# Chunk 3's attention value product as a Strassen product in two 64-row streams, with six squares on ScalarE

## The chip, the cores and the metric

One core of a Trainium2 chip runs the whole program. The metric is the time of one execution on the device in microseconds (us). The profile comes from one execution more, recorded by the hardware profiler; its instructions are told by engine: PE is TensorE's matmuls, PEld its weight loads, DVE is VectorE, ACT is ScalarE, POOL is GpSimd, SP is SyncE, which here issues DMAs.

## The reference

Eight batches of 3008 tokens. `u` and `v` have 256 channels, `z` has 64.

```python
scores = (1.0 / S) * np.matmul(z, z.transpose(0, 2, 1))
attn = np.maximum(scores, 0.0) ** 2
out = np.matmul(attn, v)
x = (u * out).reshape(B * S, D)                 # 24064 x 256
h = x @ w_in                                    # 256 x 2048
g = h * (1.0 / (1.0 + np.exp(-1.702 * h)))
y = g @ w_out                                   # 2048 x 256
```

The score matrix of a batch is symmetric, since both of its factors are `z`.

## The kernel before, in words

**Tiling.** A batch has 24 key blocks of 128 tokens (the last holds 64) and 6 query chunks of 512 tokens (`NCH = 6`, `CH = 512`; the last has 448 for some purposes). Two key blocks are one unit, so a unit `(i, jp)` is the scores of query chunk `i` against key blocks `2 jp` and `2 jp + 1`: a tile of 128 x 2 x 512. Only units on and above the diagonal are computed. What lies below it comes out of them by a DMA transposition (`turn_unit`, issued on SP's queue), whose result lies in `TT[b, i, cj]`, four blocks by four blocks. The unit on the diagonal is folded: its second half is transposed into the tile `ad`.

**A unit's way.** `scores` has PE make a pair of 64-row matmuls (line 247) into a PSUM tile of pool `ps2` (two buffers); `square` has ScalarE apply Relu into `rl` (line 268, 258 or 263) and VectorE square it into `a` (lines 282, 285, 273, 259, 264); then the DMA transposition follows. `take(b, n)` does this for the next `n` units of the queue. `SCHED` says at which step `n` of which chunk a unit is taken: during chunk `i`, mostly units of chunk `i + 1`, and the order inside a chunk comes from `pieces`.

**The value product.** `attend(b, i)` gives the list of steps of chunk `i`. In chunks 0 to 3 and 5, the 128 rows of PE are used as two halves of 64 rows, `TOP` and `LOW`, which work at the same time. A step is a pair of matmuls of 64 rows by 512 columns (line 529): first channel half 0 from the top rows and channel half 1 from the low rows over 23 key blocks, then the last block's half, then the same with the halves exchanged; 47 pairs. The two halves write different PSUM banks (pool `ps1`, four banks). When they exchange banks, PE must know that the other half's last matmul has landed: `post` puts an instruction on POOL that waits for it, and `behind` makes the next matmul wait for that instruction. At the end of a chunk, two gates (line 546) multiply the two banks with the transposed `u` on VectorE and give `XT[b, i]`.

**Chunk 4** of batches 1 to 6 (`split`) is already a Strassen product in Winograd's form: `attend_split` runs seven products `P1` to `P7`, each over three pairs of key chunks `t` (line 440, 128 rows by 256 columns), into three PSUM banks. `P6`, `P7` and `P4` are accumulated on the bank of `P1`, and `P3` on that of `P5`, after a copy or an addition has taken the value so far out. The sums of values `VT` (`value_forms`, line 363) and of scores `SA` (`score_forms`, lines 383 to 396: `S1` to `S4`) are made on VectorE at the steps that `fills` lists as `(chunk, step)`.

**The second part.** From step 2 of chunk 4, `up_group` interleaves the first 16 groups of the up product (line 584): PE makes `hg`, ScalarE applies Gelu into `gf` (line 597, two buffers), and the scaling of `gf` into `g` is VectorE's (line 603) or in some groups ScalarE's (line 601). The other groups and the down product, again a Strassen product (line 757), follow after chunk 5. `store` transposes a result on VectorE (line 859) and writes it with four DMAs on SP. `turn_u` transposes `u` on VectorE (line 214), at the steps that `TURNS` lists; `load_u` loads it through POOL's queue.

**Order.** All five engines' orders are written out by hand: an engine runs its instructions in the order in which the program issues them, and a tile pool of n buffers makes the first writer of a buffer wait for the last reader of the tile before.

Of the kernel before, what the change touches and what calls it, by code (L numbers as in the profile page):

```python
# [11 lines left out]
P = 128  # L12
# [3 lines left out]
def kernel(  # L16
# [210 lines left out]
    def folded(b, i):  # L227

        return i < NCH - 1 and b > 0
# [5 lines left out]
    def scores(b, group):  # L235
        scs = []
        zt = ZT[b]
        for i, jp in group:
            sc = ps2.tile([P, 2, CH], F32, name="sc", tag="ps2")
            turn = turned(b, i) and jp >= NU - 2  # L240
            kp, qi = (2 * i + jp - (NU - 2), NCH - 1) if turn else (jp, i)
            q0, q1 = qi * CH, qi * CH + width(qi)
            if jp == 2 * i + 1 and (folded(b, i) or i == NCH - 1):
                q0 += CH // 2
            for r in range(2):
                h = slice(r * DQK, (r + 1) * DQK)
                pe.matmul(  # L247
                    sc[:, r, :q1 - q0], zt[h, 2 * kp + r, :], zt[h].rearrange("d n p -> d (n p)")[:, q0:q1],
                    start=True, stop=True,
                )  # L250
            scs.append(sc)
        return [lambda u_=u_, sc=sc: square(b, *u_, sc) for u_, sc in zip(group, scs)]

    def square(b, i, jp, sc):
        rl = pw.tile([P, 2, CH], F16, name="rl", tag="rl", bufs=3)
        if folded(b, i) and jp == 2 * i + 1:
            rh = rl[:, :, :CH // 2]
            act.activation(rh, sc[:, :, :CH // 2], AF.Relu, scale=csc)
            dve.tensor_tensor(unit[b, i, jp][:, 1], rh, rh, ALU.mult)
            return  # L260
        if i == NCH - 1 and jp == NU - 1:
            n = LAST - CH // 2
            act.activation(rl[:, :, :n], sc[:, :, :n], AF.Relu, scale=csc)
            dve.tensor_tensor(unit[b, i, jp][:, :, CH // 2:LAST], rl[:, :, :n], rl[:, :, :n], ALU.mult)
            return
        turn = jp >= NU - 2 and (turned(b, i) or i == NCH - 1)
        n = width(NCH - 1 if turn else i)
        act.activation(rl[:, :, :n], sc[:, :, :n], AF.Relu, scale=csc)  # L268
        if folded(b, i) and jp == 2 * i:
# [11 lines left out]
        unit[b, i, jp] = a  # L281
        dve.tensor_tensor(a[:, :, :n], rl[:, :, :n], rl[:, :, :n], ALU.mult)  # L282
        if turn:
            twice = rl[:, :, LFULL:LAST]
            dve.tensor_tensor(a[:, :, LAST:], twice, twice, ALU.mult)
        if i == NCH - 1 and jp == NU - 2:
# [13 lines left out]


    ORDER0 = [(0, 1), (0, 2), (1, 2), (0, 3), (1, 3), (2, 3), (0, 4), (1, 4), (2, 4), (3, 4)]
    squared = {}
# [62 lines left out]

    def score_part(b, t, e, part, m):

        i, c0 = NCH - 2, 2 * t + e
        if c0 == i:  # L370
            if part == 0:
                return unit[b, i, 2 * i][:, 2 * m:2 * m + 2]
            return unit[b, i, 2 * i + 1][:, m].rearrange("p r (q c) -> p r q c", c=P)
        tile_ = TT[b, min(c0, i), max(c0, i)][:, 2 * m:2 * m + 2]
        if t < NCH // 2 - 1:
            return tile_.rearrange("p q g c -> p (q g c)")
        tile_ = tile_[:, :, 2 * part:2 * part + 2]
        return tile_ if part == 0 else tile_.rearrange("p q r c -> p r q c")

    def score_form(b, t, name, part):  # L380
        a11, a12, a21, a22 = (score_part(b, t, e, part, m) for m, e in ((0, 0), (0, 1), (1, 0), (1, 1)))
        if name == "S3":
            dve.tensor_tensor(a21, a11, a21, ALU.subtract)
            return
        if (t, name) not in SA:
            SA[t, name] = pa.tile([P, 2, CH], F16, name="sa", tag="a", bufs=26)
        if t < NCH // 2 - 1:
            view = lambda x: SA[t, x].rearrange("p r c -> p (r c)")
        else:
            view = lambda x: SA[t, x][:, part].rearrange("p (q r c) -> p q r c", r=2, c=P)  # L390
        if name == "S1":
            dve.tensor_tensor(view(name), a21, a22, ALU.add)
        elif name == "S2":
            dve.tensor_tensor(view(name), view("S1"), a11, ALU.subtract)
        else:
            dve.tensor_tensor(view(name), a12, view("S2"), ALU.subtract)

    def score_forms(b, t):
        parts = 1 if t < NCH // 2 - 1 else 2
        return [lambda x=x, p_=p_: score_form(b, t, x, p_) for x in ("S1", "S2", "S4", "S3") for p_ in range(parts)]  # L400

    def moving(b, t, g, name):

        raw = {"P1": (0, 0), "P2": (0, 1), "P4": (1, 1), "P7": (1, 0)}
        if name in raw:
            m, e = raw[name]
            i, c0 = NCH - 2, 2 * t + e
            if c0 != i:
                return TT[b, min(c0, i), max(c0, i)][:, 2 * m:2 * m + 2, g]
            if g < 2:  # L410
                return unit[b, i, 2 * i][:, 2 * m:2 * m + 2, g]
            return unit[b, i, 2 * i + 1][:, m, g % 2]
        form = SA[t, {"P5": "S1", "P6": "S2", "P3": "S4"}[name]]
        if t < NCH // 2 - 1:
            return form.rearrange("p r c -> p (r c)").rearrange("p (q g c) -> p q g c", g=CB, c=P)[:, :, g]
        part = form[:, g // 2].rearrange("p (q r c) -> p q r c", r=2, c=P)
        return part[:, :, g % 2] if g < 2 else part[:, g % 2]

# [7 lines left out]
    def attend_split(b, i):  # L426

        seq = [("P1", 0), ("P1", 1), ("P1", 2), ("P5", 0), ("P5", 1), ("P2", 0), ("P2", 1), ("P6", 0), ("P6", 1)]
        seq += [("P5", 2), ("P6", 2), ("P3", 0), ("P3", 1), ("P7", 0), ("P7", 1), ("P7", 2)]
# [4 lines left out]
        def step(name, t, h):  # L434
# [4 lines left out]
            for g in (2 * h, 2 * h + 1):  # L439
                pe.matmul(  # L440
                    bank, still(b, t, g, name), moving(b, t, g, name),
                    start=new and (t, g) == (0, 0), stop=(t, g) == (2, CB - 1), skip_group_check=True,
                )
# [20 lines left out]
        return [lambda x=x, t=t, h=h: step(x, t, h) for x, t in seq for h in range(2)]  # L464

    def fills(b):

        VT.clear()
        SA.clear()
        at = {(0, 19): [lambda: pool.tensor_copy(VZ[TOP], V16[b][TOP, NJ - 1])]}  # L470
        slots = [(0, n) for n in (20, 23, 26, 28)] + [(1, n) for n in (27, 31, 35, 39, 43)]
        slots += [(2, n) for n in (19, 21, 23)]
        ops = [op for t in range(3) for op in value_forms(b, t)]
        slots += [(2, n) for n in (28, 33, 38, 43)] + [(3, n) for n in (30, 34, 41, 44)]
        slots += [(4, n) for n in (8, 9, 11, 12, 14, 15, 17, 18)]
        ops += [op for t in range(3) for op in score_forms(b, t)]
        assert len(ops) == len(slots)
        for where, op in zip(slots, ops):
            at.setdefault(where, []).append(op)
        return at  # L480
# [88 lines left out]
    def up_group(b, q):  # L569
# [28 lines left out]
        if pair and q >= LAGY:  # L598
            some_sums(3 if q % 2 else 8)
        if q >= LAGY and q % 8 in (1, 3, 5):  # L600
            act.activation(g, gf[:, :, :n], AF.Copy, scale=FSC)  # L601
        else:
            dve.tensor_scalar(g, gf[:, :, :n], FSC, None, ALU.mult)  # L603
# [273 lines left out]
    def pieces(b, i):  # L877
# [6 lines left out]
        if split(b, i):  # L884
            return [lst[0], lst[3], lst[2], lst[1]]
        k = max(len(lst) - 6, 2)
        return lst[:k] + lst[-2:] + lst[k:-2]
# [3 lines left out]
        0: {n: 1 for n in (5, 9, 13, 17, 30, 33, 36, 39, 42, 45)} | {NJ: 2},  # L891
        1: {n: 1 for n in (5, 9, 13, 17)} | {NJ: 2},
        2: {n: 1 for n in (2, 7, 12, 17)} | {NJ: 2},
        3: {n: 1 for n in (3, 10, 17, 38)} | {NJ: 2},
        4: {},
# [7 lines left out]
    TURN = {(1, NJ + 4): 2, (2, NJ + 4): 3, (4, 10): 4, (5, 8): 5}  # L903
    TURNS = {(1, NJ + 4): 2, (2, NJ + 4): 3, (4, 20): 4, (5, 8): 5}
    LOADW = {
# [18 lines left out]
    def take(b, n):  # L924
        for post_ in scores(b, [queue.pop(0) for _ in range(n)]):
            post_()

# [22 lines left out]
    copies = first_zt(2)  # L950
    posts[0]()
    first_cast(3)
    posts[1]()
    take(0, 1)
# [4 lines left out]
    for b in range(B):  # L959
# [7 lines left out]
        for i in range(NCH):  # L967
# [4 lines left out]
            if i == 0 and split(b, NCH - 2):  # L972
                extra = fills(b)
            for n, step in enumerate(attend_split(b, i) if split(b, i) else attend(b, i, b == 0 and i == 0)):
                if b == 0 and i == 0 and n in (5, 24):
# [9 lines left out]
                if (i, n) in turn:  # L985
                    turn_u(b, turn[i, n])
                if (i, n) in ((3, 4), (4, 1) if more else (4, 14)) and LAST2:
                    LAST2.pop(0)()
# [92 lines left out]
```

## Time and profile before

| | |
|---|---|
| median of 3 runs | 1170.55 us (1170.28 to 1172.03) |
| the profiled execution's own time | 1170.41 us |
| its span, first to last instruction | 1168.5 us |
| PE busy | 1161.9 us, 8212 matmuls |
| VectorE busy | 958.7 us, 1596 instructions |
| ScalarE busy | 842.1 us, 959 instructions |
| POOL busy | 224.3 us |
| DMA transpositions into `tt` | 232 issues, 3.4 us from issue to landing in the median |

The page gives an engine's busy time as a share of the span, and cuts the span into 40 slices with the granted clock of TensorE. Busy times of matmuls overlap (each is shown longer than the distance to the next), so the pace of PE is read from the starts of instructions that follow each other. A chain of waits is followed back from the last instruction of the program. Batch 2, whose chunks 0 to 4 lie between 303.5 and 372.8 us of the span, serves as the example.

### The profile page before, as it was taken

The page shows a single profiled execution, that of the slowest core. Times are in us where ns is not written, and L with a number is a line of the kernel's source. Part 1 is how long each engine was busy: PE and PEld are TensorE (multiplying, and loading weights), DVE is VectorE, ACT ScalarE, POOL GpSimd, SP SyncE. Part 2 cuts the span into 40 slices and gives each one's busy share as a digit, 9 for nine tenths or more (in the row PEclk, how much of TensorE's full clock was granted, in tenths as well). Part 3 has the DMA queues.
Part 4 walks back from the last instruction along what each step waited for, and adds up shares of the span by engine and source line. Part 5 has one row for each costly group of instructions (what it writes and reads, how often), then busy time and mean ns, then how long its engine had stood idle before and what let it go on. Part 6 is the DMA issues. An engine that isn't in the chain of part 4 may idle for free.

```text
span 1168.5 us, 21541 instructions
## 1 busy us (share of the span) xinstructions
PE 1161.9 (99%) x8212; PEld 589.5 (50%) x8212; DVE 958.7 (82%) x1596; ACT 842.1 (72%) x959; POOL 224.3 (19%) x307
## 2 busy tenths in 40 slices
PE   9999999999999999999999999999999999999998
PEld 3544455544455445554445545555444554544446
DVE  7789878988788886889868897789977899664876
ACT  7888864788647886478864787658867588672785
POOL 3033200432004320042101431024210251001000
PEclk9999999999999999999999999999999999999999
DMA  9996399754996559875498755987559965697023
GB/s 225 202 155 107 79 172 158 105 91 92 166 158 103 91 109 172 146 111 87 96 173 146 114 88 109 170 149 104 87 107 174 145 108 81 123 162 139 1 37 73
DMA packets 459033, 143.54 MB, mean 123 GB/s; under 512 B 424624, under 2 KB 453040, under 8 KB 458928
## 3 DMA queue, kind: packets, MB, share of 16 engines
q1 hardware_dynamic: 402464, 102.36, 52.4%
q0 software_dynamic: 55104, 38.49, 21.1%
q8 instruction: 64, 1.05, 0.4%
q10 hardware_dynamic: 1360, 1.31, 0.4%
q14 instruction: 41, 0.34, 0.1%
HBM read 60.29 MB, written 24.64 MB: 73 GB/s over the span
## 4 chain that ended last, share of the span: by engine, by line
PE 99%; ACT 1%; issue 0%; DVE 0%
PE o L529 36%; PE hg L584 28%; PE st L757 23%; PE sc L247 6%; PE oz L440 5%; PE st L805 1%; PE yp L731 1%; ACT rl L268 0%; PE w L101 0%; ACT ZT L145 0%; PE zp L137 0%; DVE y L823 0%; ACT zst L128 0%; DVE nil L76 0%
## 5 line engine op out<-in xcount | busy, mean ns | idle before, releaser
L597 ACT ACTIVATE gf<-hg 128x1024 f32<-128x1024 f32 (+1 forms) x384 | 383.8, 1003 | 116.3 <-PE hg L584 100.5
L268 ACT ACTIVATE rl<-sc 128x1024 f16<-128x1024 f32 (+1 forms) x301 | 288.6, 992 | 153.7 <-PE sc L247 112.8
L584 PE MATMUL hg<-xt,W 128*128 128x512 f16 (+1 forms) x1408 | 353.5, 374 | 0.0
L529 PEld LDWEIGHTS <-V 64*128 64x128 f16 (+1 forms) x3810 | 205.9, 94 | 202.7 <-POOLq L88 6.6
L529 PE MATMUL o<-a,V 64*128 64x512 f16 (+3 forms) x2254 | 290.2, 368 | 0.4 <-DVE a L282 0.4
L603 DVE TENSOR_SCALAR gt<-gf 128x1024 f16<-128x1024 f32 (+1 forms) x288 | 203.1, 708 | 72.0 <-ACT gf L597 70.1
L282 DVE TENSOR_TENSOR a<-rl 128x1024 f16<-128x1024 f16 (+1 forms) x266 | 175.9, 672 | 80.1 <-ACT rl L268 79.0
L584 PEld LDWEIGHTS <-W 128*128 128x128 f16 x1536 | 149.6, 98 | 155.7 <-issue 2.6
L207 POOL DMA_DIRECT2D uq<-in_u_dram x168 | 120.7, 728 | 341.1 <-DVE ut L214 157.6
L529 PE MATMUL o<-tt,V 64*128 64x512 f16 (+1 forms) x1278 | 166.9, 376 | 0.1
L247 PE MATMUL sc<-ZT 64*128 64x512 f16 (+3 forms) x688 | 117.0, 356 | 0.6 <-ACT ZT L145 0.3
L757 PEld LDWEIGHTS <-WT 128*128 128x128 f16 x736 | 72.0, 98 | 79.5 <-issue 0.6
L601 ACT ACTIVATE gt<-gf 128x1024 f16<-128x1024 f32 (+1 forms) x96 | 98.1, 1021 | 3.1
L757 PE MATMUL st<-gt,W 128*128 128x512 f16 (+1 forms) x368 | 89.9, 370 | 0.0
L757 PE MATMUL st<-s,WT 128*128 128x512 f16 (+1 forms) x368 | 89.1, 370 | 0.0
L757 PE MATMUL st<-gt,WT 128*128 128x512 f16 (+1 forms) x368 | 88.7, 370 | 0.0
L993 POOL COPY hold<-tt 128x2 f16<-128x2 f16 x6 | 1.4, 230 | 430.1 <-DMA tt<-a 287.4
L757 PEld LDWEIGHTS <-W 128*128 128x128 f16 x552 | 53.8, 98 | 58.2
L774 DVE SCALAR_TENSOR_TENSOR y<-st,y 128x512 f32<-128x512 f32 (+1 forms) x69 | 45.8, 663 | 19.7 <-PE st L757 18.8
L721 DVE TENSOR_TENSOR s<-s,gt 128x1024 f16<-128x1024 f16 (+1 forms) x92 | 60.5, 657 | 0.8
L723 DVE TENSOR_TENSOR s<-gt,s 128x1024 f16<-128x1024 f16 (+1 forms) x92 | 59.4, 662 | 2.0 <-DVE s L721 0.9
L719 DVE TENSOR_TENSOR s<-gt 128x1024 f16<-128x1024 f16 (+1 forms) x92 | 60.2, 659 | 0.9
(101 smaller groups left out, 975.7 us busy)
## 6 DMA issues: line engine op xcount, KB each, us to landing
out_dram<-yo SPq DMA_DIRECT2D x156, 128.0 KB, 2.8
uq<-in_u_dram POOLq DMA_DIRECT2D x140, 128.0 KB, 3.5
V<-in_v_dram POOLq DMA_DIRECT2D x35, 256.0 KB, 6.1
tt<-a SPq DMA_TRANSPOSE x232, 3.4
uq<-in_u_dram POOLq DMA_DIRECT2D x28, 112.0 KB, 5.0
out_dram<-yo SPq DMA_DIRECT2D x28, 96.0 KB, 3.3
uq<-in_u_dram SPq DMA_DIRECT2D x20, 128.0 KB, 4.3
wst<-in_moe_w_in_dram POOLq DMA_DIRECT2D x4, 512.0 KB, 5.3
```

Of the source, the lines that this page charges most:

```text
L207: eng.dma_start(uq[k * QW:(k + 1) * QW, :n // QW].rearrange("t q c k -> t q (c k)"), src[:, :, cs])
L247: pe.matmul(sc[:, r, :q1 - q0], zt[h, 2 * kp + r, :], zt[h].rearrange("d n p -> d (n p)")[:, q0:q1], start=True, stop=True,)
L268: act.activation(rl[:, :, :n], sc[:, :, :n], AF.Relu, scale=csc)
L282: dve.tensor_tensor(a[:, :, :n], rl[:, :, :n], rl[:, :, :n], ALU.mult)
L529: ins = pe.matmul(acc[c][:, :n], channels(V16[b][h, j], c), weights(b, i, j)[h], start=(k, m) == first[c], stop=(k, m) == final[c],)
L584: pe.matmul(hg[:, e, :n], W1[:, c, ff * P:(ff + 1) * P], XT[b, i][:, c, :n], start=(c == 0), stop=(c == NCC - 1),)
L597: act.activation(gf[:, :, :n], hg[:, :, :n], AF.Gelu_apprx_sigmoid, scale=1.0 / FSC)
L601: act.activation(g, gf[:, :, :n], AF.Copy, scale=FSC)
L603: dve.tensor_scalar(g, gf[:, :, :n], FSC, None, ALU.mult)
L719: dve.tensor_tensor(s_, a21, a22, ALU.add)
L721: dve.tensor_tensor(s_, ST[b, s, "S1", m], a11, ALU.subtract)
L757: pe.matmul(bank, right[:, ff], lhs[:, f], start=new and ff == 0, stop=ff == NFF // 2 - 1, skip_group_check=True,)
```

## The change

In batches 1 to 6, chunk 3 (`NCH - 3`) gets its own function `attend_rows`. It is a Strassen product like chunk 4's, but in 64-row mode: the low and the top rows each run a stream of 21 steps, `ROWL` and `ROWT`, which go through the seven products and the three pairs of key chunks in different orders. A step `(name, t)` is four slots, and a slot is one matmul of 256 columns in each stream, both at once. Four PSUM banks `W`, `X`, `Y`, `Z` hold the products (`HOME`). A product's six parts (three `t`, two row halves) accumulate in one bank, and wherever it passes from one stream to the other a `post` and a `behind` stand between. When a product is complete, ScalarE copies it (`P1`, `P7`, `P4`, part of `P6`) or VectorE adds it to a copied part (`P5`, `P2`, and at the end `P6` and `P3`); two multiplications with `u` end the chunk.

The sums of scores for chunk 3 (`near`) come on top of those for chunk 4 (`far`), and `fills` lists new steps for all of them and for the sums of values. Six squares per batch (`SQUARES`, and the small second part of the turned ones) go from VectorE to ScalarE, and so do two scalings of `gf` (groups 9 and 13). In `take`, all Relus of a call are now issued before its squares. `P2` goes ahead of `P5` in chunk 4's first steps. The steps of units in chunks 1 to 3, the order of chunk 3's units, two of `u`'s transpositions and one store are moved.

```diff
+    def relu(b, i, jp, sc):
+        rl = pw.tile([P, 2, CH], F16, name="rl", tag="rl", bufs=3)
...
+        act.activation(rl[:, :, :n], sc[:, :, :n], AF.Relu, scale=csc)
+        return lambda: square(b, i, jp, rl)
...
-        dve.tensor_tensor(a[:, :, :n], rl[:, :, :n], rl[:, :, :n], ALU.mult)
+        by_act = rowed(b, NCH - 3) and (i, jp) in SQUARES
+        if by_act:
+            act.activation(a[:, :, :n], rl[:, :, :n], AF.Square)
+        else:
+            dve.tensor_tensor(a[:, :, :n], rl[:, :, :n], rl[:, :, :n], ALU.mult)
...
+    SQUARES = ((2, 6), (2, 8), (2, 9), (3, 9), (3, 11), (5, 10))
...
+    def rowed(b, i):
+
+        return i == NCH - 3 and 0 < b < B - 1
...
-        seq = [("P1", 0), ("P1", 1), ("P1", 2), ("P5", 0), ("P5", 1), ("P2", 0), ("P2", 1), ("P6", 0), ("P6", 1)]
+        seq = [("P1", 0), ("P1", 1), ("P1", 2), ("P2", 0), ("P2", 1), ("P5", 0), ("P5", 1), ("P6", 0), ("P6", 1)]
...
+    ROWT = [("P1", 0), ("P1", 1), ("P1", 2), ("P2", 0), ("P7", 0), ("P7", 1), ("P7", 2), ("P5", 0), ("P5", 1), ("P5", 2)]
+    ROWT += [("P6", 0), ("P6", 1), ("P6", 2), ("P4", 0), ("P4", 1), ("P4", 2), ("P2", 1), ("P2", 2)]
+    ROWT += [("P3", 0), ("P3", 1), ("P3", 2)]
+    ROWL = [("P7", 0), ("P7", 1), ("P7", 2), ("P5", 0), ("P1", 0), ("P1", 1), ("P1", 2), ("P2", 0)]
+    ROWL += [("P4", 0), ("P4", 1), ("P4", 2), ("P5", 1), ("P5", 2), ("P2", 1), ("P2", 2), ("P3", 0), ("P3", 1), ("P3", 2)]
+    ROWL += [("P6", 0), ("P6", 1), ("P6", 2)]
+    HOME = {"P1": "X", "P6": "X", "P7": "W", "P4": "W", "P5": "Y", "P3": "Y", "P2": "Z"}
+
+    def attend_rows(b, i):
+
+        streams = ((LOW, ROWL), (TOP, ROWT))
...
+        def step(k, h):
+            for g in (2 * h, 2 * h + 1):
+                for r, (rows_, seq) in enumerate(streams):
+                    name, t = seq[k]
+                    home = HOME[name]
+                    fresh = home not in banks
+                    if fresh:
+                        banks[home] = ps1.tile([P, CH], F32, name="oz", tag="ps1")
+                    ins = pe.matmul(
+                        banks[home][:, :half], still(b, t, g, name)[rows_], moving(b, i, t, g, name)[rows_],
+                        start=fresh, stop=(k, g) == (ends[name], CB - 1), skip_group_check=True,
+                    )
+                    if name in sigs and sigs[name][0] != r:
+                        behind(sigs.pop(name)[1], ins)
+                    last[r] = name, ins
+            if h:
+                for r in range(2):
+                    name, ins = last[r]
+                    if leaves(k, r, name):
+                        sigs[name] = r, post([ins])
+                for name in sorted((n for n in ends if ends[n] == k), reverse=True):
+                    evacuate(name)
+
+        def evacuate(name):
...
+            if name in ("P1", "P7", "P4"):
+                act.activation({"P1": c11, "P7": c22, "P4": c21}[name], bank, AF.Copy, scale=1.0)
+            elif name == "P5":
+                dve.tensor_tensor(c22, c22, bank, ALU.add)
+            elif name == "P2":
+                dve.tensor_tensor(c11, c11, bank, ALU.add)
+            elif name == "P6":
+                dve.tensor_tensor(c21, c21, bank, ALU.add)
+                act.activation(c12, bank, AF.Copy, scale=1.0)
+                dve.tensor_tensor(c22, c22, bank, ALU.add)
+                dve.tensor_tensor(x[:, 0], y[0][:, 0], ut(0), ALU.mult)
+                dve.tensor_tensor(c12, c12, banks["Y"][:, :half], ALU.add)
+                dve.tensor_tensor(x[:, 1], y[0][:, 1], ut(1), ALU.mult)
...
-        slots = [(0, n) for n in (20, 23, 26, 28)] + [(1, n) for n in (27, 31, 35, 39, 43)]
-        slots += [(2, n) for n in (19, 21, 23)]
-        ops = [op for t in range(3) for op in value_forms(b, t)]
-        slots += [(2, n) for n in (28, 33, 38, 43)] + [(3, n) for n in (30, 34, 41, 44)]
-        slots += [(4, n) for n in (8, 9, 11, 12, 14, 15, 17, 18)]
-        ops += [op for t in range(3) for op in score_forms(b, t)]
+        near, far = NCH - 3, NCH - 2
+        put(0, (20, 23, 26, 28, 34, 37, 40, 43), value_forms(b, 0) + value_forms(b, 1))
+        put(1, (14, 20, 27, 31), value_forms(b, 2))
+        put(1, (35, 38, 41, 44), score_forms(b, near, 0))
+        put(2, (20, 21, 25, 26, 28, 31, 32), score_forms(b, near, 1, ("S1", "S2", "S3", "S4")))
+        put(2, (38, 39), score_forms(b, near, 2, ("S3",)))
+        put(3, (2, 2, 10, 11, 16, 18), score_forms(b, near, 2, ("S1", "S2", "S4")))
+        put(3, (28, 30, 32, 37), score_forms(b, far, 0))
+        put(4, (3, 5), score_forms(b, far, 1, ("S1", "S2")))
+        put(4, (9, 10, 12, 13), score_forms(b, far, 2, ("S1", "S2")))
+        put(4, (15, 20), score_forms(b, far, 1, ("S4", "S3")))
+        put(4, (17, 18, 22, 23), score_forms(b, far, 2, ("S4", "S3")))
...
-        if q >= LAGY and q % 8 in (1, 3, 5):
+        if (q >= LAGY and q % 8 in (1, 3, 5)) or (split(b, NCH - 2) and q in (9, 13)):
             act.activation(g, gf[:, :, :n], AF.Copy, scale=FSC)
...
+        if rowed(b, i):
+            return [lst[0], lst[5], lst[1], lst[4], lst[2], lst[3]]
...
-        1: {n: 1 for n in (5, 9, 13, 17)} | {NJ: 2},
-        2: {n: 1 for n in (2, 7, 12, 17)} | {NJ: 2},
-        3: {n: 1 for n in (3, 10, 17, 38)} | {NJ: 2},
+        1: {n: 1 for n in (4, 10, 16, 36)} | {NJ: 2},
+        2: {n: 1 for n in (2, 7, 13, 19)} | {NJ: 2},
+        3: {n: 1 for n in (3, 8, 15, 21, 28, 36)},
...
-    TURNS = {(1, NJ + 4): 2, (2, NJ + 4): 3, (4, 20): 4, (5, 8): 5}
+    TURNS = {(1, NJ + 4): 2, (2, 10): 3, (4, 25): 4, (5, 8): 5}
...
-                if (i, n) in ((3, 4), (4, 1) if more else (4, 14)) and LAST2:
+                if (i, n) in ((3, 4), (4, 7) if more else (4, 14)) and LAST2:
```

In the last lines `n` counts a chunk's steps; in the new chunk 3 a step of the product counts as two, of two slots each, 42 in all.

## The prediction

> **What bounds the kernel now.** I read the page first (busy time, slices, chain), then the chain in order of time for the pace of one matmul, then stretches of batch 2 for the other engines.
>
> ```profile
> PE 1161.9 (99%) x8212; PEld 589.5 (50%) x8212; DVE 958.7 (82%) x1596; ACT 842.1 (72%) x959; POOL 224.3 (19%) x307
> PEclk9999999999999999999999999999999999999999
> PE 99%; ACT 1%; issue 0%; DVE 0%
> ```
>
> TensorE is busy throughout and alone makes the chain; the clock is full. A busy PE need not be at its peak, so the pace decides:
>
> ```profile
> 303.50 1.08 PE o L529 x10
> 438.80 1.23 PE yp L731 x22
> 352.85 0.60 PE L440 MATMUL oz<-sa,vt 128*128 128x256 f16 x4
> 353.29 1.03 PE L584 MATMUL hg<-xt,W 128*128 128x512 f16 x4
> 347.67 0.26 PE L247 MATMUL sc<-ZT 64*128 64x192 f16 x2
> 347.75 0.83 PE L529 MATMUL o<-tt,V 64*128 64x512 f16 x6
> ```
>
> Columns: start, length, what. Five pairs of 64-row matmuls of 512 columns take 1.08 us, 0.216 a pair. Four 128-row matmuls of 256 columns start at 352.85 and the next kind at 353.29: 0.109 each. Line 731 has 128 columns and 0.056 each. A 64-row pair of 192 columns gives way to the next pair after 0.08. So PE sends columns without a hole: what leaves its stream shortens the kernel, and any new wait lengthens it.
>
> ```profile
> core 0: us, PE busy (x) PEld busy (x) DVE busy (x) ACT busy (x) POOL busy (x), PEclk, DMA share, GB/s
> 303.50:316.60 13.10, 13.10 (x128) 6.23 (x124) 10.42 (x19) 12.57 (x15) 0.00 (x0) 1.00 0.97 183
> 316.60:327.60 11.00, 11.00 (x106) 5.84 (x104) 8.65 (x16) 5.95 (x7) 0.00 (x0) 1.00 0.99 168
> 327.60:338.70 11.10, 11.10 (x108) 5.93 (x106) 10.39 (x22) 5.39 (x6) 0.00 (x0) 1.00 1.03 156
> 338.70:349.80 11.10, 11.10 (x108) 5.65 (x103) 9.86 (x19) 4.76 (x6) 0.00 (x0) 1.00 0.80 148
> 349.80:372.80 23.00, 23.00 (x150) 14.39 (x148) 20.71 (x35) 16.20 (x18) 11.47 (x15) 1.00 0.85 132
> ```
>
> These are chunks 0 to 4 of batch 2. VectorE has 1 to 2 us to spare in each, ScalarE 5 to 6 in chunks 1 to 3, and POOL is empty in chunks 0 to 3.
>
> **What PE gains.** Chunk 3 had 23 + 1 + 23 = 47 pairs of 512 columns: 47 x 0.216 = 10.15 us. It gets 21 steps of 4 slots, each a pair of 256 columns: 84 x 0.109 = 9.16. Score pairs between (six) and mode switches stay. That is -1.0 a chunk, -5.9 over six batches (unrounded paces). The trace has no long run of 64-row pairs of 256 columns, where two loads and two matmuls share 0.109. Bounds: 0.109, which the 192-column pair undercuts (two loads and two matmuls in 0.08), and 0.112, two of line 731's load-and-matmul: 84 x 0.112 = 9.41, -4.4 in all. I take 0.109, being the nearer row.
>
> The row says 0.056 for load and matmul together. The Trainium skill, "TensorE: Matmul & The Clock Gate", section "Back-to-back issue gap", gives about 81 ns for each load-matmul pair at 128 columns; two per slot would be 162 ns, 84 of them an estimated 13.6 us a chunk, and the kernel near 1191 us. The row contradicts it here, and nothing else below uses it.
>
> **What it adds beside PE, per batch.** Instructions on one engine overlap, so a queue advances by starts, not by lengths:
>
> ```profile
> 348.81 0.68 DVE L396 TENSOR_TENSOR sa<-tt,sa 128x1024 f16<-128x1024 f16 x1
> 349.42 0.68 DVE L383 TENSOR_TENSOR tt<-tt 128x1024 f16<-128x1024 f16 x1
> 350.02 1.28 DVE L546 TENSOR_TENSOR xt<-o,ut 128x512 f16<-128x512 f32 x2
> L452 ACT ACTIVATE ya<-oz 128x256 f32<-128x256 f32 x18 | 6.8, 378 | 0.0
> ```
>
> 0.60 us for a whole sum (a half one 0.33: two in chunk 4 start at 356.54 and 356.87), 0.60 for a gate, 0.38 for a copy of 256 columns. VectorE gets 19 more sums of scores (5 whole, 14 halves: 7.6) and five additions out of PSUM (1.7), less six squares (3.7) and two scalings (1.3). Net +4.3 on 143 us. ScalarE: six squares and two scalings at about 1.0 (line 601's scaling takes 1.06), four copies of 0.38: +9.6 or so. A square out of SBUF has no row; 0.9 to 1.06 bounds it. These hide behind PE if their queues keep up: chunk 2 loses 2.5 us of VectorE work (its later-chunk sums, value sums and two squares), chunk 0 gets four value sums (2.4, nearly filling it; the spill goes into chunk 1, where three squares leave), chunk 3 gets about 2.5, chunk 4 about 1. Without that cover each late microsecond on VectorE in chunk 3 or 4 is one on PE. The spill of chunk 0 delays its gates by about 2 us; their banks are wanted again only in chunk 2, 10 us on. Transpositions stay 297 in number; the order of chunk 3's pieces changes on SP's queue. Of the moved steps, u's transpositions (chunk 2, step 28 to 10; chunk 4, 20 to 25) and a store (chunk 4, step 1 to 7, with its 1.25 on VectorE and four DMAs on SP) keep their cost and lie where (d) and (e) count them; P2 and P5 of chunk 4 trade places on the same 0.109.
>
> **The new waits on PE, per batch.** Nothing passes a waiting matmul: both streams and the score pairs behind it stop.
>
> (a) Handing a bank from one row stream to the other goes through a POOL instruction. The price:
>
> ```profile
> 1070.73 0.81 PE L529 MATMUL o<-tt,V 64*128 64x512 f16 x6
> 1071.38 0.25 PE L247 MATMUL sc<-ZT 64*128 64x192 f16 x2
> 1071.65 0.33 PEld L529 LDWEIGHTS <-V 64*128 64x128 f16 x6 [0.39 <-POOLq L88]
> ```
>
> The last pair before the turn starts at 1071.16 (the third of 1070.73), the matmul that waited at 1071.65: 0.49, less half a pair's 0.216 for 256 columns: 0.38. Each handover but one has a whole step between (0.109 + 4 x 0.109 = 0.55), so costs nothing while POOL is empty. P3 goes from the low stream (step 17) to the top one (step 18) with one score pair between: 0.109 + 0.08 = 0.19 of cover, 0.19 of wait. Bounds 0 (if POOL answered at once) and 0.30 (0.49 without the deduction).
>
> (b) P4 is added on P7's bank after ScalarE has copied it. The last matmul of P7 to copy start: 0.35 (a 512-column score pair to its relu is 0.46, less 0.11); the copy 0.38; back to PE 0.05: 0.78. Step 7 and the score pair in it give 0.109 + 0.436 + 0.19 = 0.735. Wait 0.05; 0 to 0.9 if a relu (0.92) stands in front.
>
> (c) P3 starts on P5's bank after VectorE's addition. PE gets there 7.4 us into the chunk. VectorE has before it, in order: two gates from 0.2 (1.2), two half sums (0.66), a square (0.6, 0.3 late behind its relu), the transposition for a store (1.25), square 0.67, halves 0.66, square 0.67, halves 0.66, half square 0.33, the addition 0.33: 7.5. Wait 0.1; 0 to 1.5 (the first rival).
>
> (d) P2 and P5 open on chunk 2's banks at step 3. Last matmul of chunk 2 to its second gate's end: 0.44 + 0.60 + 0.68 = 1.72; PE is there after 0.216 + 3 x 0.436 + 0.216 + 0.109 = 1.85. That needs VectorE without arrears at the end of chunk 2 (it had about one now). 0.05; 0 to 0.5.
>
> (e) Chunk 4: two whole sums early, two later, two scalings on ScalarE; chunk 3's last additions hold VectorE until about 2.7 us into the chunk, as gates and store do now. 0.05; 0 to 0.5.
>
> Together 0.44, times six 2.6. Sum: -5.9 + 2.6 = -3.3. The profiled execution took 1170.41 (span 1168.5), which is 0.14 under the median 1170.55: 1170.4 - 3.3 = **1167.1**.
>
> **Rivals.**
>
> *VectorE late in chunk 3 (the other sign).* The first half sums there, at step 2, need the transposition of chunk 3's piece 10, now third of its run on SP, whose issues stand close:
>
> ```profile
> 333.36 1.21 SPq L275 DMA_TRANSPOSE ad<-a  x1
> 334.67 5.51 SPq L310 DMA_TRANSPOSE tt<-a  x4
> ```
>
> Four in 5.51 is 1.38 each; the second of these goes at 336.0 and lands after 3.7, at 339.7; VectorE asks at 338.7 + 1.4 = 340.1. Margin 0.4. If it lands later, or the arrears of chunk 2 remain, everything in (c) moves. A lateness L beyond mine costs 6 L: 1167.1 + 6 L, over 1172.9 from L = 0.97; with 1.5 us, 1176. For it: VectorE at 9.9 of 11.1 in the chunk now and more to come. Against: chunk 2's relief and that margin.
>
> *The pairs run slower than 0.109.* At 0.112 the sum is 1168.6, no measurable change; break-even with waits is a slot of about 0.116. For it: no such run in the trace; against: the 192-column pair.
>
> *All waits covered.* Only (a) at 0.1 remains: -5.9 + 0.6, 1165.1. *The shorter chunk brings nothing*, the next stage waiting for VectorE or ScalarE instead: 1170.4, for which chunk 4's 20.7 of 23.0 speaks; PE waits for neither there now.
>
> **How the numbers follow.** 0.2% is 2.3 us, about what a measurement of this kernel can tell from no change: faster is under 1168.2, slower over 1172.9. My forecast 0.47, covered waits 0.15, both faster: 0.62. Slow pairs 0.06 and nothing gained 0.11: same, 0.17. VectorE late by over 0.97, with a pace worse than any row: 0.21 slower. The likeliest case alone spans 1165.1 to 1168.6; the range goes from 1165.1 to 1174.0 (L = 1.15), leaving about 0.05 below and 0.15 above.
>
> **What would show it.** Right: 256-column pairs starting 0.109 apart on the new matmul line, chunk 3 at about 10.6 us with its score pairs (11.1 now), one bubble near 0.2 at step 18 released by POOL, PE's other idle under 0.3 a batch. Wrong: slots of 0.115 or more; bubbles at steps 8, 10 or 15 released by ScalarE or VectorE; VectorE's sums waiting for a transposition; Gelu or the scalings holding PE in chunk 4.

## The result and the profile after

The changed kernel takes 1172.72 us in the median of 11 runs (1171.84 to 1174.59), the kernel before 1170.40 in the same comparison; the ratio is 1.0019, with a 95% interval from 1.0010 to 1.0028. That is 2.3 us slower, where 3.3 us faster was forecast. It lies inside the range, on the wrong side of no change. The profiled execution has 1172.72 us and a span of 1170.4 (1168.5 before).

The page after, its busy times and the first line of the chain that ended last:

```profile
PE 1161.1 (99%) x8656; PEld 611.3 (52%) x8656; DVE 983.6 (84%) x1680; ACT 894.9 (76%) x1043; POOL 224.4 (19%) x307
PE 84%; DVE 11%; ACT 2%; issue 2%; DMA 1%; DVEq 0%; ACTq 0%
```

The chain was PE for 99%; now 11% of it is VectorE. PE's busy share hardly shows this, since it counts overlapping lengths.

Chunks 0 to 4 of batch 2, as before (columns as there):

```profile
303.40:316.50 13.10, 13.10 (x126) 6.25 (x124) 10.67 (x20) 12.57 (x15) 0.00 (x0) 1.00 1.08 182
316.50:327.40 10.90, 10.90 (x105) 5.74 (x103) 10.80 (x22) 8.91 (x10) 0.00 (x0) 1.00 1.05 164
327.40:338.50 11.10, 11.10 (x108) 6.01 (x106) 9.61 (x20) 7.49 (x9) 0.00 (x0) 1.00 1.14 166
338.50:348.90 10.40, 10.40 (x182) 9.37 (x178) 9.75 (x22) 6.72 (x11) 0.00 (x0) 1.00 0.70 123
348.90:373.40 24.50, 23.65 (x151) 14.38 (x148) 23.73 (x40) 18.03 (x22) 11.69 (x15) 1.00 0.83 129
```

Chunk 3 is 10.4 us long instead of 11.1. Chunk 4 is 24.5 instead of 23.0, VectorE is busy for 23.73 of it, and for the first time PE is not busy throughout a stretch.

The new matmuls, and the one handover that was to cost something (timelines of PE, then of its weight loads):

```profile
347.04 0.27 PE L541 MATMUL oz<-sa,V 64*128 64x256 f16 x1
347.06 0.27 PE L541 MATMUL oz<-tt,V 64*128 64x256 f16 x1
347.15 0.27 PE L541 MATMUL oz<-sa,VZ 64*128 64x256 f16 x1
347.17 0.27 PE L541 MATMUL oz<-tt,VZ 64*128 64x256 f16 x1
347.26 0.26 PE L247 MATMUL sc<-ZT 64*128 64x192 f16 x2
347.34 0.27 PE L541 MATMUL oz<-sa,vt 64*128 64x256 f16 x1
347.53 0.28 PE L541 MATMUL oz<-sa,V 64*128 64x256 f16 x1
347.53 0.28 PE L541 MATMUL oz<-sa,vt 64*128 64x256 f16 x1
```

```profile
347.52 0.09 PEld L541 LDWEIGHTS <-V 64*128 64x128 f16 x1 [0.17 <-POOLq L88]
347.65 0.09 PEld L541 LDWEIGHTS <-V 64*128 64x128 f16 x1
347.65 0.09 PEld L541 LDWEIGHTS <-vt 64*128 64x128 f16 x1
```

A slot is two of these lines, one for each stream. The pairs start 0.11 apart (347.04, 347.15), with two weight loads each. The handover takes 0.38, from the low stream's last matmul of `P3` at 347.15 to the top stream's first at 347.53, and the instruction on POOL releases it.

To compare many runs I use one more number. A *hole* is the time by which a matmul starts later than the pace of the one before it allows (0.216, 0.109 or 0.056 us), read from the starts in the trace, from 103 us on. Delays up to 25 ns and changes between 64 and 128 rows (0.09 each, as before) are not counted. Before: 0.39 us in all. After: 8.10, of which 0.65 in the six chunks 3 (0.11 each) and 7.26 in the six chunks 4 (0.89, 1.47, 0.89, 1.97, 0.88 and 1.15). PE's own stream is 5.85 shorter at the unrounded paces: 1168.5 - 5.85 + 8.10 - 0.39 = 1170.4, the span that was measured. (The same sum meets the spans of the other runs to within 0.9 us.) So the whole gain came, and more than the whole of it was lost in chunk 4.

The largest hole of batch 2, on three engines (timeline):

```profile
363.60 0.38 PE L483 MATMUL oz<-tt,vt 128*128 128x256 f16 x2
364.62 0.59 PE L706 MATMUL hg<-xt,W 128*128 128x512 f16 x2 [0.64 <-ACT gf L719]
361.38 1.02 ACT L719 ACTIVATE gf<-hg 128x1024 f32<-128x1024 f32 x1 [0.53 <-DVE gt L725]
363.55 1.97 ACT L719 ACTIVATE gf<-hg 128x1024 f32<-128x1024 f32 x2 [0.87 <-PE hg L706]
359.38 1.30 DVE L432 TENSOR_TENSOR sa<-sa,ad 128x512 f16<-128x512 f16 x1
360.61 0.68 DVE L725 TENSOR_SCALAR gt<-gf 128x1024 f16<-128x1024 f32 x1
361.21 1.64 DVE L436 TENSOR_TENSOR sa<-tt,sa 128x1024 f16<-128x1024 f16 x2
362.78 0.68 DVE L725 TENSOR_SCALAR gt<-gf 128x1024 f16<-128x1024 f32 x1
```

PE waits for a Gelu (line 719). The Gelu at 363.55 is put down to PE, whose matmuls had long been made; it starts when the scaling of 362.78 (line 725) has freed one of the two `gf` buffers. That scaling stood behind sums of scores (lines 432 and 436) in VectorE's queue. The view of waits for chunk 4 has the same: ScalarE's Gelu for VectorE's scaling, 3.6 us in five waits, where before it was PE that Gelu waited for.

```profile
ACT gf L719 <- DVE gt L725: 3.6, 5, 1.0
ACT gf L719 <- PE hg L706: 1.3, 2, 0.9
```

```profile
ACT gf L597 <- PE hg L584: 7.4, 13, 3.0
```

The first is of the kernel after, the second of the kernel before (total, times, longest).

### The profile page after: what moved, and what is told of

Its sections match the earlier page's. It is cut to its first block, busy times and chain, and to the rows that moved or that the text cites. A ratio compares the mean times of both kernels' runs of the same rounds, so it can differ in the third digit from the quotient of the medians.

```text
span 1170.4 us, 22657 instructions
## 1 busy us (share of the span) xinstructions
PE 1161.1 (99%) x8656; PEld 611.3 (52%) x8656; DVE 983.6 (84%) x1680; ACT 894.9 (76%) x1043; POOL 224.4 (19%) x307
## 3 DMA queue, kind: packets, MB, share of 16 engines
q10 hardware_dynamic: 1360, 1.31, 0.4%
## 4 chain that ended last, share of the span: by engine, by line
PE 84%; DVE 11%; ACT 2%; issue 2%; DMA 1%; DVEq 0%; ACTq 0%
PE o L651 29%; PE st L879 23%; PE hg L706 23%; PE sc L247 5%; DVE gt L725 3%; PE oz L483 1%; DVE sa L436 1%; ACT rl L260 1%; PE st L927 1%; DVE sa L430 1%; DMA tt<-a 1%; DVE yo L981 1%; PE yp L853 1%; DVE sa L432 1%; DVE tt L418 1%
## 5 line engine op out<-in xcount | busy, mean ns | idle before, releaser
L260 ACT ACTIVATE rl<-sc 128x1024 f16<-128x1024 f32 (+1 forms) x344 | 310.8, 941 | 132.1 <-PE sc L247 113.1
L651 PE MATMUL o<-a,V 64*128 64x512 f16 (+3 forms) x2110 | 271.8, 368 | 0.2 <-DVE a L291 0.2
L651 PEld LDWEIGHTS <-V 64*128 64x128 f16 (+1 forms) x3246 | 174.5, 94 | 174.3 <-issue 5.5
L725 DVE TENSOR_SCALAR gt<-gf 128x1024 f16<-128x1024 f32 (+1 forms) x276 | 193.6, 705 | 59.4 <-ACT gf L719 57.8
L291 DVE TENSOR_TENSOR a<-rl 128x1024 f16<-128x1024 f16 (+1 forms) x230 | 152.2, 670 | 65.7 <-ACT rl L260 64.6
L651 PE MATMUL o<-tt,V 64*128 64x512 f16 (+1 forms) x906 | 119.4, 376 | 0.0
L723 ACT ACTIVATE gt<-gf 128x1024 f16<-128x1024 f32 (+1 forms) x108 | 110.7, 1025 | 3.6
```

Source lines behind the costliest of these rows:

```text
L651: ins = pe.matmul(acc[c][:, :n], channels(V16[b][h, j], c), weights(b, i, j)[h], start=(k, m) == first[c], stop=(k, m) == final[c],)
```

## The experiments

All are made from the changed kernel, except the last control. Times are medians of 4 to 11 executions, ratios are to the kernel before on the same chip. The holes are those of the one profiled execution.

| run | time, us | ratio, 95% | holes, us |
|---|---|---|---|
| the change | 1172.72 | 1.0019 (1.0010 to 1.0028) | 8.10 |
| four sums less | 1165.47 | 0.9962 (0.9948 to 0.9976) | 0.84 |
| scalings back | 1178.46 | 1.0069 (1.0054 to 1.0084) | 14.20 |
| two more scalings moved | 1169.56 | 0.9999 (0.9990 to 1.0008) | 5.19 |
| old product, new schedule | 1179.03 | 1.0070 (1.0055 to 1.0085) | 7.36 |
| z's copies on ScalarE | 1169.71 | 0.9991 (0.9982 to 1.0000) | 5.18 |
| z's copies on ScalarE, and group 5 | 1176.09 | 1.0041 (1.0026 to 1.0056) | 10.69 |
| early sums | 1182.81 | 1.0105 (1.0088 to 1.0122) | 18.25 |
| early sums, and two scalings | 1177.22 | 1.0064 (1.0042 to 1.0087) | 12.49 |
| group 3 moved | 1171.47 | 1.0001 (0.9993 to 1.0010) | 6.84 |
| z's copies, 13 alone | 1167.28 | 0.9968 (0.9957 to 0.9979) | 2.22 |
| z's copies, 3 and 13 | 1167.25 | 0.9976 (0.9965 to 0.9986) | 3.93 |
| the kernel before, z's copies | 1170.13 | 0.9999 (0.9990 to 1.0009) | 0.19 |

### Is it VectorE's load in chunk 4?

Theory V: VectorE has too much to do there. Theory S: ScalarE is too slow, with two scalings and the new copies.

**Four sums less.**

```diff
-        form = SA[i, t, x]
+        form = SA[i, 0 if i == NCH - 2 and t == 1 else t, x]
...
-        put(4, (3, 5), score_forms(b, far, 1, ("S1", "S2")))
-        put(4, (15, 20), score_forms(b, far, 1, ("S4", "S3")))
```

> The four whole sums of scores for chunk 4's second pair of key chunks (S1, S2, S4, S3 of t = 1) are left out in batches 1 to 6; the products that would read them read the first pair's instead, so the output is not the reference's and only VectorE loses work (4 x 0.60 us a batch). Theory V (VectorE has too much to do in chunk 4, Gelu waits for its scalings, PE for Gelu): the holes of TensorE in chunk 4, 7.3 us over six batches in the changed kernel, nearly all go: 1165.5 to 1167 us. Theory S (ScalarE is too slow there, with two scalings and the new copies): the holes stay, 1172 to 1173 us.

1165.47 us, holes 0.84: theory V, to the microsecond. PE's stream is what it is in the changed kernel and ScalarE has the same instructions. So 2.4 us of VectorE's work a batch stood between the change and its whole gain. Chunk 4 of batch 2 takes 23.1 us, as in the kernel before, VectorE is busy for 21.15 of it, and no Gelu waits for a scaling (columns of the stretch as above; view of waits: total, times, longest):

```profile
348.24:371.35 23.11, 23.11 (x149) 14.40 (x149) 21.15 (x37) 18.68 (x22) 11.77 (x15) 1.00 0.89 135
```

```profile
ACT gf L717 <- PE hg L704: 2.9, 8, 0.5
DVE gt L723 <- ACT gf L717: 1.4, 4, 0.5
```

**Scalings back, and two more moved.**

```diff
-        ... (split(b, NCH - 2) and q in (9, 13)):
+        ... (split(b, NCH - 2) and q in ()):
```

> Groups 9 and 13 are scaled by VectorE again, nothing else is changed. Theory V: 1.3 us more on VectorE in a chunk 4 that has none to spare, up to 1.3 us a batch more: 1175 to 1181 us. Theory S: ScalarE is relieved of 2.1 us a batch, Gelu comes earlier: 1166 to 1170 us.

```diff
-        ... (split(b, NCH - 2) and q in (9, 13)):
+        ... (split(b, NCH - 2) and q in (3, 5, 9, 13)):
```

> Groups 3 and 5 are scaled by ScalarE as well as 9 and 13. Theory V: VectorE is relieved of 1.3 us a batch before the holes, they shrink by more than half: 1167 to 1170 us. Theory S: two more microseconds on ScalarE a batch, 1174 to 1182 us.

1178.46 and 1169.56: both go the way of theory V. Two scalings are worth 5.7 us over six batches on the one side and 3.2 on the other. Not all of the 5.7 lies in chunk 4. Of the 6.1 us of holes that "scalings back" has more than the change, 2.1 are there, 2.4 are at score pairs just behind it in chunk 5 (0.40 a batch), where the chain of batch 2 goes through a late Gelu, and 1.6 are one wait for a transposed tile in the last batch. On the other side the holes of chunk 4 shrink to 4.4, not by the half that was expected, because new ones appear at groups 4 to 6, where ScalarE now has scalings between its Gelus. ScalarE was a relief, not the bound.

### Which part of the change fills chunk 4?

```diff
-        put(1, (35, 38, 41, 44), score_forms(b, near, 0))
-        put(2, (20, 21, 25, 26, 28, 31, 32), score_forms(b, near, 1, ("S1", "S2", "S3", "S4")))
-        put(2, (38, 39), score_forms(b, near, 2, ("S3",)))
-        put(3, (2, 2, 10, 11, 16, 18), score_forms(b, near, 2, ("S1", "S2", "S4")))
...
-                attend_split(b, i) if split(b, i) else attend_rows(b, i) if rowed(b, i)
+                attend_split(b, i) if split(b, i) else attend(b, i) if rowed(b, i)
```

> Chunk 3 of batches 1 to 6 by the pairs of before, without the sums of scores that its Strassen product needs; every other part of the change stays (steps, squares and scalings on ScalarE, chunk 4's sums at their new places). PE's stream is 5.8 us longer, and the exchange of banks in chunk 3 has no score pair beside it any more, up to 1.6 us. If chunk 4's holes come from the sums that were moved into it, they stay: 1177 to 1180 us. If they come from what the new product leaves to VectorE at the end of chunk 3, they go: 1171 to 1174 us.

1179.03 us, the first case. Of its 7.36 us of holes, 1.61 are the six exchanges of banks in chunk 3 (0.27 each, no score pair beside them); 5.5 stay in chunk 4. So most of chunk 4's loss comes from what the change puts there, not from the product. The run with four sums less leaves out the ones that lay in chunk 3 before, keeps the new product, and has no hole left in chunk 4. The two runs together name these sums. The store and a transposition of `u` that the change moves inside chunk 4 stay in both runs; no run moves them back alone, but without the four sums they make no hole. The rest, 1.8 us by difference, goes with the new product; that it is the additions with which it holds VectorE at the end of chunk 3 is argued, not shown.

### What makes VectorE's sums long

Some sums of 0.41 us are shown with 1.30 and 1.04 (the second of the two at 361.21). POOL's two copies of `z` for the next batch (line 174) run just then (timeline of POOL):

```profile
359.56 0.83 POOL L174 COPY zst<-zst 128x768 f16<-128x768 f16 x1
361.58 1.00 POOL L174 COPY zst<-zst 128x768 f16<-128x768 f16 x1 [1.18 <-DMA zst<-in_z_dram]
```

The edit moves them to ScalarE, at steps 24 and 29, and with each the transposition that follows it on SP's queue:

```diff
-            pool.tensor_copy(zst[:, :, 1, :], zst[:, :, 0, :])
...
+    def turn_z(b, n0, copy):
...
+        copy(zst[:, :, 1, :], zst[:, :, 0, :])
+        sp.dma_start_transpose(ZT[b][:, n0:n0 + NU], zst.rearrange("p n c d -> p (n c d)"))
...
+                if more and b and (i, n) in ((NCH - 2, 24), (NCH - 2, 29)):
+                    turn_z(b + 1, NU * int(n == 29), lambda o, x: act.activation(o, x, AF.Copy, scale=1.0))
```

> The two copies of z that POOL makes in chunk 4 of batches 1 to 6 (about 0.9 us each) are made by ScalarE, at steps 24 and 29. In the changed kernel, two VectorE sums that ran beside them took 1.30 and 1.04 us instead of 0.41. Theory P (POOL's copies hold VectorE up, by 1.2 us a batch): no such long sum is left, and PE's holes shrink by about as much as two sums are worth: 1167 to 1170 us. Theory W (the long sums are waits for something else and only shown as length): the long sums stay, and the time stays at 1172 to 1174 us, since VectorE gets no time back.

1169.71 us, in the range of theory P, and the long sums are gone (timeline of VectorE, the same two lines of code, now 436 and 440):

```profile
359.18 0.41 DVE L436 TENSOR_TENSOR sa<-sa,ad 128x512 f16<-128x512 f16 x1
359.52 0.68 DVE L729 TENSOR_SCALAR gt<-gf 128x1024 f16<-128x1024 f32 x1
360.12 1.02 DVE L440 TENSOR_TENSOR sa<-tt,sa 128x1024 f16<-128x1024 f16 x2
```

A whole and a half sum together take 1.02 here, 1.64 before the edit. The Trainium skill, "SBUF — State Buffer", section "SBUF: two separate sides", says that a VectorE instruction with two SBUF inputs and a GpSimd instruction that reads SBUF exclude each other for a whole instruction, since they share a pair of ports. The traces agree in part. In batches 1 to 6 of the changed kernel each of the twelve copies stands beside one VectorE instruction lengthened by about 0.6 to 0.9 us, and none of these is left when ScalarE copies. Ten of them are sums with two inputs in SBUF; the two of batch 5 are scalings (1.31 us where others take 0.68), which have one such input and which that sentence does not cover. One or two scalings a batch also take 0.96 to 1.2 us while POOL issues the loads of `z` (line 160), with and without the copies; no run takes these away.

The control asks whether the copies cost anything by themselves:

> The control: the kernel before, with z's copies moved from POOL to ScalarE in the same way, and nothing of the change. TensorE has no hole in its chunk 4 to fill. If the copies are worth time only where VectorE's lateness reaches TensorE: 1170 to 1171.5 us, no gain. If moving them is worth 3 us by itself, whatever the rest: 1167 to 1168 us.

1170.13 us against 1170.40: no gain. The kernel before has lengthened instructions too, such as this half sum, but VectorE's lateness did not reach PE there:

```profile
361.65 1.04 DVE L383 TENSOR_TENSOR ad<-ad 128x512 f16<-128x512 f16 x1
```

### Where ScalarE becomes the bound

Group 5 scaled by ScalarE in addition (`q in (5, 9, 13)`):

> As the run before, and group 5 is scaled by ScalarE besides 9 and 13. Theory V with P: VectorE has 1.2 + 0.65 us a batch less to do, nearly what leaving out four sums saved: 1165.5 to 1168 us. If ScalarE becomes the limit instead (18.0 of 24.5 us before, 21 after): 1169 us or more, with PE's holes released by Gelu that waits for nothing.

1176.09 us: the other case, and worse than without it. ScalarE has Gelu, scaling, Gelu and copy in a row, and PE waits 0.54 us for the second Gelu (timelines of ScalarE, then PE):

```profile
361.23 1.06 ACT L727 ACTIVATE gt<-gf 128x1024 f16<-128x1024 f32 x1
362.19 1.00 ACT L723 ACTIVATE gf<-hg 128x1024 f32<-128x1024 f32 x1
363.25 1.02 PE L710 MATMUL hg<-xt,W 128*128 128x512 f16 x4 [0.54 <-ACT gf L723]
```

Over chunk 4 (24.7 us) ScalarE is busy for only 20.6 us. But in each of the three largest holes of batch 2 (0.70, 0.39 and 0.35 us) the Gelu that PE waits for follows ScalarE's instruction before it without a pause, and VectorE in turn waits for Gelu for 2.1 us, where it was 0.7 with the copies alone. It is the place that counts.

Squares to ScalarE and two sums back into chunk 3:

```diff
-    SQUARES = ((2, 6), (2, 8), (2, 9), (3, 9), (3, 11), (5, 10))
+    SQUARES = ((2, 6), (2, 8), (2, 9), (3, 9), (3, 11), (4, 10), (4, 11), (5, 10))
...
-        put(4, (3, 5), score_forms(b, far, 1, ("S1", "S2")))
+        put(3, (33, 34), score_forms(b, far, 1, ("S1", "S2")))
```

> Two more squares a batch (units 10 and 11 of chunk 4) go to ScalarE, and S1 and S2 of chunk 4's second pair are made in chunk 3 (steps 33 and 34), not in chunk 4 (steps 3 and 5). VectorE's work in chunk 3 stays as it was (1.3 us less, 1.2 more) and chunk 4 has 1.2 us less. Theory V: about half to three quarters of the holes go, 1167 to 1169.5 us. If it is the end of chunk 3 that counts and not the load of chunk 4: no gain, 1172 us or more.

1182.81 us: a miss for theory V, with no hole gone and 10 us more. The other case, "1172 us or more", covers the number, but not for its reason. The squares (lines 289 and 295) stand in ScalarE's order before the copy of P7 (line 564) and before a relu. Timelines of ScalarE and of PE in that run:

```profile
344.16 0.95 ACT L289 ACTIVATE a<-rl 128x896 f16<-128x896 f16 x1
345.02 0.29 ACT L295 ACTIVATE a<-rl 128x128 f16<-128x128 f16 x1
345.22 0.64 ACT L564 ACTIVATE yr<-oz 128x256 f32<-128x256 f32 x2
```

```profile
344.84 0.27 PE L541 MATMUL oz<-sa,vt 64*128 64x256 f16 x1
345.63 0.27 PE L541 MATMUL oz<-tt,vt 64*128 64x256 f16 x1 [0.53 <-ACT yr L564]
```

PE stops for 0.69 at step 8, waiting for the copy (the second timeline above), which is wait (b) with a square in front. VectorE then stands idle for 2.2 us behind the late relu (the view of waits), so chunk 4 begins later for VectorE, not earlier (chunk 3 holds it until 4.5 us into chunk 4, and 3.5 without the edit):

```profile
DVE ad L266 <- ACT rl L260: 2.2, 1, 2.2
```

The run moved load and order at once and says nothing on the load alone.

> As the run before, and groups 3 and 5 are scaled by ScalarE besides 9 and 13. Theory V: VectorE's chunk 4 is 2.5 us a batch lighter than in the changed kernel, as much as with four sums left out: the holes go, 1165 to 1166.5 us, under both kernels, with the right output. If ScalarE is then the limit: 1168 us or more.

1177.22 us, with the same 0.69 in every chunk 3: a miss for theory V, and again only the open range of the other case covers it. Against the run before, two scalings moved give back 5.6 us, which is theory V once more, on a worse start.

### A version that beats both

Group 3 alone in addition, without the copies:

> Group 3 is scaled by ScalarE besides 9 and 13 (with 3 and 5 besides it was 1169.6 us, its holes at groups 4 to 6 released by ScalarE). VectorE gets 0.65 us a batch back, in the part of chunk 4 before its holes. Theory V: 1168 to 1170 us. If one scaling more is not enough for VectorE: 1170 to 1172 us.

1171.47 us (1169.24 to 1172.00), the second case: one scaling more is not enough for VectorE, 6.84 us of holes are left. The spread of its runs reaches both kernels, so the run settles nothing else.

Then z's copies on ScalarE, and 9 back on VectorE:

> z's copies on ScalarE as in the earlier run (1169.7 us), and group 9 is scaled by VectorE again, so only 13 is ScalarE's. The holes left there, 0.15 and 0.35 us a batch about steps 31 to 35, stood beside ScalarE's copy and scaling in a row with no pause between its Gelus. If ScalarE's queue makes them, they go: 1166.5 to 1168.5 us. If VectorE does, it has 0.65 us more to do: 1171 to 1174 us.

1167.28 us, ratio 0.9968 (0.9957 to 0.9979): 3.2 us under the kernel before on the same chip (1170.46) and 5.4 under the changed one, 0.2 from the time that was forecast for the change. ScalarE's queue had made the last holes of the run with the copies; without group 9 it has room for them. Chunk 4 of batch 2 is down to 23.3 us:

```profile
348.50:371.80 23.30, 23.30 (x150) 14.38 (x148) 22.53 (x42) 18.52 (x23) 10.61 (x13) 1.00 0.83 137
```

With group 3 moved too:

> z's copies on ScalarE, and groups 3 and 13 scaled by ScalarE (with 13 alone it was 1167.3 us, 2.2 us of holes left, about half of them near groups 4 to 6 in the batches 2, 4 and 6). VectorE gets 0.65 us a batch back before them. If they were VectorE's: 1166 to 1167 us. If ScalarE is full there: 1168 us or more.

1167.25 us: the same, between the two cases. Its profiled execution (1168.44 us) has more holes, 3.93, but 2.02 of them are one wait in the last batch, far from the change, where PE waits for a transposed tile:

```profile
1069.02 1.04 PE L655 MATMUL o<-tt,V 64*128 64x512 f16 x8 [1.86 <-DMA tt<-a]
```

Its six chunks 4 have 1.1 us of holes, against 1.4 in the run before. Whether this last microsecond is VectorE's or ScalarE's stays open.

## Why the prediction was wrong, step by step

*What PE gains* was right: pairs 0.11 apart, chunk 3 at 10.4 us (10.6 said), 5.85 us less of stream. The 81 ns that the Trainium skill, "TensorE: Matmul & The Clock Gate", section "Back-to-back issue gap", gives for a load-matmul pair at 128 columns did not show in the long run of 64-row pairs either: two loads and two matmuls of 256 columns go in 109 ns.

*Waits (a) to (d)* were forecast at 0.39 a batch and measured 0.11. In (a), 0.38 for the handover was exact, but the low stream's own slot of 0.109 also ran in its shade, which the sum left out: the hole is 0.08, not 0.19. At (b) it was 0.03 (0.05 said), but the run with more squares shows it reach 0.69 when one stands in front. At (c) and (d) there was none. For (c) VectorE made what was listed, in that order, with P5's addition last:

```profile
345.35 0.42 DVE L566 TENSOR_TENSOR yr<-yr,oz 128x256 f32<-128x256 f32 x1
```

It starts 6.9 us into the chunk, where the list gives 7.2, and ends 0.18 us before PE is there (345.95). That is close, and the rival "VectorE late in chunk 3" did not come about.

*Wait (e) failed*, "Chunk 4: two whole sums early, two later, two scalings on ScalarE", put at 0.05 a batch with 0.5 as its upper bound. It measured 1.21 on average, up to 1.97. Two things were wrong in it. First, the load: "chunk 4 about 1" was to bring VectorE from 20.7 to 21.7 of 23.0 us, and it is busy for 23.7. Counted from start to start in the two timelines, these 3.0 us more are 2.5 for the four sums less 1.5 for two scalings, which is the 1 that was said; 1.5 for the end of chunk 3; and 0.7 for sums lengthened by POOL's copies (smaller items take 0.2 off). The end of chunk 3 (its last sum, three additions, two multiplications) holds VectorE until 3.5 us into chunk 4, and the store, which was inside the 2.7 that were said, comes after that, among the scalings:

```profile
351.70 0.69 DVE L575 TENSOR_TENSOR xt<-yr,ut 128x512 f16<-128x512 f32 x1
355.10 1.23 DVE L981 STREAM_TRANSPOSE yo<-y 128x1024 f32<-128x1024 f32 x1
```

The prediction's own terms had a spill in them: chunk 3 stood at 9.9 us of VectorE, was to get 2.5 more and to last 10.6, and with about one of arrears less that still leaves nearly a microsecond for chunk 4. The copies it read past in the trace of before, where a half sum of 0.42 stood with 1.04. Second, the rule: an engine with a microsecond to spare in 23 was taken as cover enough. Between VectorE and PE there are two `gf` buffers and Gelu, so as the timelines read it is not the load over the stretch that counts but any run of sums that delays a scaling by more than the pause in Gelu (about 0.28 to 0.5 us before). No run gives `gf` a third buffer, so this link is read from the trace and not tested by itself.

*The rivals.* The one that came is "the shorter chunk brings nothing, the next stage waiting for VectorE or ScalarE instead", with 0.11 of the chances and the row that spoke for it, 20.7 of 23.0. Its time, no change, was still 2.3 us too low: the loss in chunk 4 was larger than the gain, as the sums moved there cost it even with the old product. So the case that ended slower was priced in the wrong chunk, for VectorE late in chunk 3, and it is luck that this makes the range reach up to the measured time. Among the signs of being wrong, "Gelu or the scalings holding PE in chunk 4" is the one that came.

## What to carry to other kernels

Where one engine sends without a hole, a shorter stream on it is a gain that can be counted (all of the 5.85 us came here) and every other engine's queue a possible loss: price each moved instruction by where it stands in its queue, and look for the short buffer chain (here two `gf` tiles) through which it comes back. An engine at 90% of a stretch is not cover for work added in one place, and moving load to the freer engine pays only where its own order has a pause. Look at the longest of equal instructions, not only at their mean: what lengthens them may cost nothing until the load rises.

## What the runs showed of the hardware

A copy on POOL of 128 x 768 elements from SBUF to SBUF lengthened the VectorE instruction beside it by 0.6 to 0.9 us, ten times a sum and twice a scaling; moved to ScalarE (0.83 us there), it lengthened none. In the kernel before, VectorE's transpositions beside such a copy kept their 1.23 us. A long run of 64-row pairs of 256 columns, with two weight loads for each pair, keeps 0.109 us a pair. A square of 128 x 1024 from SBUF takes ScalarE 1.06 us, and 0.95 for 896, as long as the scaling and no less than a relu out of PSUM.
